# Gating the experts in transposed layout, with the gates of four chunks sent once through DRAM

## Chip, core and metric

The kernel runs on one core of one Trainium2 chip. The metric is the device time of one launch in microseconds (us). The engines are TensorE (PE: matmuls and transposes; PEld is its weight loads), VectorE (DVE), ScalarE (ACT), GpSimd (POOL) and SyncE (SP), which here only issues DMAs. DMAs are issued from SP's, ACT's and POOL's queues.

## The reference, cut to what matters

Attention over pooled keys, then two of eight low-rank experts per token. B=4, 12288 query tokens per batch, C=128, 768 pooled keys per batch, E=8 experts of rank 16.

```python
kv_pool = kv.reshape(B, H//4, 4, W//4, 4, C).mean(axis=(2, 4))
k = v = kv_pool.reshape(B, -1, C) @ w_sr
s = (q @ k.transpose(0, 2, 1)) / np.sqrt(C)
a = softmax(s);  x = (a @ v).reshape(-1, C)

logits = x @ w_gate                       # 8 experts, the best two kept
topk = np.argpartition(-logits, 2, axis=1)[:, :2]
w = softmax(logits of the two)
delta = sum over the two of  w * ((x @ A[e]) @ B[e])
return x + delta                          # (49152, 128) float32
```

## The kernel before, in words

The 49152 queries are cut into 96 chunks of 512 tokens (`T`), 24 chunks per batch, four chunks per group `g` of 2048 tokens (`GC`, `GT`). A chunk is four sub-tiles (`S`) of 128 tokens. The order of all instructions on each engine is the program's order (`keep`).

The main loop (L417) runs over slots `k` from 4 to 95. In slot `k`, PE computes the scores of chunk `k` in three parts (`scores`, L238: two matmuls of 512 columns each into one of two PSUM tiles `sg`), and ACT turns each part into `em` with one exp of 128x1024. The chunk before it is attended (`attend`, L248: 24 matmuls of 137 columns into `acc`, of which there is one buffer). The 137 columns are the 128 outputs, the 8 expert logits and the softmax sum. The chunk before that is normalised by DVE (`normalize`, L256: `rinv`, `xn`).

Then comes the expert part, or x stage, of a chunk. It needs `xn` and the gates of the chunk.

- Gates: for each group of chunks (`sizes`, L269: mostly four), DVE finds the sorted logits (`top`, L276), POOL makes `over`, ACT a tanh `th`, and POOL two more steps give `gw` (`route`, `gates`, L285 to L316). `gw` has tokens on partitions: 8 gates for each of the 16 sub-tiles.
- x stage: PE transposes `xn` of the chunk that enters, and in the same PSUM tile `hg` of the chunk that entered one slot before (`transposes`, L318: four and four matmuls of 128 columns); DVE copies both to `tts` (128x1024). `down` (L339) is four matmuls with the turned `x` as the weights and `a_bf` streaming, which puts tokens on partitions in `h_ps`. `gate` (L344, DVE) multiplies by `gw`, each gate broadcast over the 16 ranks of its expert. After the transpose of `hg` in the next slot, `up` (L353) is four matmuls into `d_ps`, one slot later again, and `finish` (L358, DVE) adds `xn` and issues the output DMA of 256 KB on SP.

The order of PE in a slot (L440 to L481) is: scores part 0, `transposes`, scores part 1, `up`, first quarter of `attend`, scores part 2, `down`, three quarters of `attend`. `tt_ps`, `h_ps`, `d_ps` and the tiles of the key preparation share two PSUM buffers (`mtile`).

Queries of groups 2 and up are cast to bf16 in DRAM by a DMA from POOL (`cast_q`, L77) and loaded transposed by a DMA transpose on SP (`load_qT`, L82). In such a group a sub-tile takes every sixteenth token, so that a partition's four output rows of a chunk lie side by side in DRAM. The keys and values of the next batch are loaded in slots 4 to 15 of a batch, 512 KB per slot (L430), summed by POOL in slots 10 to 20, and prepared in single steps (`rest`) in slots 14 to 23. A chunk enters the x stage as soon as its group's gates can be there (`enter`, L407 to L413); chunk 8 enters in slot 14. The last three chunks are finished in a tail written out by hand (L489 on).

Of the kernel before, what the change touches and what calls it, by code (L numbers as in the profile page):

```python
# [15 lines left out]
ALU = mybir.AluOpType  # L16
# [4 lines left out]
def kernel(  # L21
# [31 lines left out]
    qpool = ctx.enter_context(tc.tile_pool(name="qpool", bufs=4))  # L53
    ppool = ctx.enter_context(tc.tile_pool(name="ppool", bufs=7))
# [4 lines left out]
    opool = ctx.enter_context(tc.tile_pool(name="opool", bufs=6))  # L59
    qdram = ctx.enter_context(tc.tile_pool(name="qdram", bufs=1, space=bass.MemoryType.DRAM))  # L60
# [21 lines left out]
    def load_qT(g):  # L82
        t = qpool.tile([P, GT], BF16, tag="qT", name="qT")
        keep(nc.sync.dma_start(t.rearrange("c (j p) -> c j p", p=P),
                               q_bf[g].rearrange("(p j) c -> p (j c)", p=P), transpose=True))
        qT[g] = t
# [46 lines left out]
    keep(nc.sync.dma_start(b_f, moe_B.rearrange("e r c -> (e r) c")))  # L133
# [10 lines left out]
    nc.vector.tensor_copy(id_bf, id_f)  # L144
    wext = const.tile([P, VC], FP32)
# [89 lines left out]
    tts, xT, hgT, hp, hg, dp = {}, {}, {}, {}, {}, {}  # L235
    R = J // 2

    def scores(k, r):  # L238
# [7 lines left out]
        keep(nc.scalar.activation(em[k][:, 2 * r:2 * r + 2], ps, AF.Exp, bias=0.0, scale=scale))  # L246
# [22 lines left out]
    sizes = [1, 1, 2] + [GC] * (NCHUNK // GC - 5) + [2] * 4 + [1] * 8  # L269
# [13 lines left out]
    later = []  # L283
# [26 lines left out]
    def gates(k0, n, eng, arg, mask):  # L310
        th = rpool.tile([P, GC * S, 8], FP32, tag="th", name="th")[:, 0:n]
        keep(nc.scalar.activation(th, arg, AF.Tanh, bias=0.0, scale=0.5))  # L312
        w = gpool.tile([P, GC * S, 8], FP32, tag="gw", name="gw")
# [4 lines left out]
    def transposes(kx, kh):  # L318
# [14 lines left out]
        keep(nc.vector.tensor_copy(sb[:, lo:hi], ps[:, lo:hi]))  # L333
# [5 lines left out]
    def down(k):  # L339
        hp[k] = mtile([P, S, P], name="h_ps")  # L340
        for s in range(S):
            mm(hp[k][:, s], xT[k][:, s], a_bf, start=(s == 0), stop=(s == S - 1))

    def gate(k):  # L344
        k0, m = first[k], k - first[k]
        hg[k] = run.tile([P, S, P], BF16, tag="hg", name="hg")
        keep(nc.vector.tensor_tensor(  # L347
            hg[k].rearrange("p s (e r) -> p (s e) r", e=E),
            hp[k].rearrange("p s (e r) -> p (s e) r", e=E),
            gw[k0][:, m * S:(m + 1) * S].rearrange("p s e -> p (s e)")  # L350
            .unsqueeze(2).broadcast_to([P, S * E, RK]), op=ALU.mult))
# [5 lines left out]

    def finish(k):  # L358
        osb = opool.tile([P, S, C], FP32, tag="osb", name="osb")
        keep(nc.vector.tensor_tensor(osb, dp[k], xn[k][:, :, 0:C], op=ALU.add))  # L360
        keep(nc.sync.dma_start(
            out[k // GC * GT:(k // GC + 1) * GT].rearrange("(p j) c -> p j c", p=P)
            [:, k % GC * S:(k % GC + 1) * S], osb))
# [30 lines left out]
    keep(nc.vector.tensor_scalar(a_bf, a_f, 0.5, None, op0=ALU.mult))  # L394
# [12 lines left out]
    enter = {}  # L407
    e = 0
    for k in range(NCHUNK):
        done = normed[first[k] + size[k] - 1]  # L410
        two = size[k] < GC and k % 4 == 0 and len(enter.get(e, [])) < 2
        e = max(e if two else e + 1, done + 1)
        enter.setdefault(e, []).append(k)  # L413

    sums, rest = [], []
    kh, ku = [], []
    for k in range(LA, NCHUNK):  # L417
# [3 lines left out]
        if k % GC == 0:  # L421
            g = k // GC
            if 2 <= g + 1 < B * NG:
                load_qT(g + 1)
            if 4 <= g + 2 < B * NG and g + 2 not in q_bf:
                cast_q(g + 2)
        if b + 1 < B:
            if i == 4:
                sums, rest = prepare(b + 1, nc.gpsimd)
            if 4 <= i < 16:  # L430
                h, j = divmod(i - 4, 4)
                load_kv(b + 1, h, j, None)
# [12 lines left out]
        while later:  # L445
            later.pop(0)()
        for n in kn:
# [224 lines left out]
```

## Time and profile before

| what | value |
|---|---|
| time, median of 3 runs | 409.08 us (408.81 to 409.26) |
| the profiled execution, its own time | 409.56 us |
| its span on the core | 407.6 us |
| granted TensorE clock, mean | 0.991 |
| instructions | 11369 |
| DMA packets, bytes moved | 71319, 76.45 MB |
| share of SP's DMA queue / POOL's DMA queue in the time of 16 DMA engines | 53.8% / 16.7% |

The profiled execution took 2.0 us more than its span; that is start and end outside the core's first and last instruction. A timeline row gives the start in us from the span's start, the length, the engine, the line, the operation, output and input with their shapes, and the number of instructions merged into the row. PE's rows are pipelined: each ends later than the next one starts, so lengths on PE are read from start to start. The square bracket at the end of a row is the time for which the engine had been idle before it, and what ended that idle time.

### The profile page before, as it was taken

What the parts mean: (1) busy time and instruction counts of PE and PEld (TensorE: products, weight loads), DVE (VectorE), ACT (ScalarE), POOL (GpSimd) and SP (SyncE); (2) the same over time, 40 slices, a digit from 0 to 9 for tenths busy, and PEclk for the clock granted to TensorE, in tenths of its full rate; (3) what the DMA queues carried; (4) which work ended last, traced back from release to release, by engine and by line L of the source; (5) the groups of instructions that cost most, each with busy time, mean ns of one, the idle gap of its engine ahead of it and who ended that gap; (6) DMA issues with size and microseconds to landing.
All of it is one profiled execution on the core that took longest, in us unless ns stands there. A gap on an engine that the chain in (4) does not pass through costs nothing.

```text
span 407.6 us, 11369 instructions
## 1 busy us (share of the span) xinstructions
PE 379.6 (93%) x4514; PEld 306.9 (75%) x4589; DVE 324.5 (80%) x948; ACT 293.1 (72%) x346; POOL 170.7 (42%) x289
## 2 busy tenths in 40 slices
PE   3798899999999999999999999999999999898992
PEld 2556778788888788888888788878888878677781
DVE  2553678888888888989888888988988888887873
ACT  2389468767678777867778877876777877665772
POOL 0010128888512319879411319879311322123342
PEclk9999999999999999999999999999999999999996
DMA  8998568984855999994855979996756548252213
GB/s 297 366 265 245 137 156 214 285 210 124 182 130 105 307 172 336 295 219 138 168 130 117 363 103 344 287 225 145 156 131 149 138 130 156 79 138 97 79 53 132
DMA packets 71319, 76.45 MB, mean 188 GB/s; under 512 B 49921, under 2 KB 50433, under 8 KB 70785
## 3 DMA queue, kind: packets, MB, share of 16 engines
q1 hardware_dynamic: 70128, 63.98, 53.8%
q0 software_dynamic: 704, 11.54, 16.7%
q8 instruction: 36, 0.59, 0.6%
q10 hardware_dynamic: 432, 0.20, 0.2%
q14 instruction: 19, 0.15, 0.1%
HBM read 50.53 MB, written 36.70 MB: 214 GB/s over the span
## 4 chain that ended last, share of the span: by engine, by line
PE 82%; DVE 7%; ACT 3%; DMA 3%; issue 2%; SPq 1%; POOL 1%; ACTq 0%; DVEq 0%; POOLq 0%
PE acc L68 34%; PE sg L68 23%; PE tt_ps L68 10%; PE h_ps L68 6%; PE d_ps L68 5%; ACT em L246 2%; DVE rinv L258 1%; DVE xn L263 1%; DMA kvr<-in_kv_dram 1%; SPq L98 1%; DMA w_sr_sb<-in_w_sr_dram 1%; PE kpT_ps L68 1%; DVE tts L333 1%; PE v_ps L68 1%; DVE hg L347 1%
## 5 line engine op out<-in xcount | busy, mean ns | idle before, releaser
L246 ACT ACTIVATE em<-sg 128x1024 f16<-128x1024 f32 x288 | 279.1, 1023 | 92.1 <-PE sg L68 59.5
L68 PE MATMUL acc<-vx,em 128*128 128x137 f16 x2280 | 171.7, 224 | 1.7 <-DVE xn L263 1.6
L68 PE MATMUL sg<-qT,kfT 128*128 128x512 bf16 x501 | 154.7, 378 | 2.7 <-ACT em L246 2.2
L68 PEld LDWEIGHTS <-em 128*128 128x128 f16 x2304 | 149.6, 98 | 4.0 <-DVE xn L263 2.2
L68 PEld LDWEIGHTS <-tts 128*128 128x128 bf16 x740 | 56.4, 98 | 45.8 <-DVE tts L333 2.1
L293 POOL TENSOR_TENSOR over<-xn,srt 128x128 f32<-128x128 f32 (+2 forms) x62 | 21.4, 365 | 157.0 <-DVE srt L281 157.0
L347 DVE TENSOR_TENSOR hg<-h_ps,gw 128x512 bf16<-128x512 f32 x93 | 64.2, 691 | 13.2 <-POOL gw L315 7.6
L263 DVE TENSOR_TENSOR xn<-acc,rinv 128x544 f32<-128x544 f32 x95 | 68.8, 725 | 3.3
L333 DVE COPY tts<-tt_ps 128x1024 bf16<-128x1024 bf16 (+1 forms) x96 | 64.4, 671 | 3.6 <-PE tt_ps L68 3.6
L171 POOL TENSOR_TENSOR kvr<-kvr 128x512 f32<-128x512 f32 x54 | 66.7, 1271 | 0.0
L360 DVE TENSOR_TENSOR osb<-d_ps,xn 128x512 f32<-128x512 f32 x91 | 62.6, 691 | 0.5 <-PE d_ps L68 0.5
L68 PEld LDWEIGHTS <-kfT 128*128 128x128 bf16 x576 | 45.9, 97 | 6.0 <-issue 3.7
L68 PEld LDWEIGHTS <-xn 128*128 128x128 bf16 x384 | 29.4, 98 | 22.0 <-ACT xn L585 0.5
L258 DVE RECIPROCAL rinv<-acc 128x4 f32<-128x4 f32 x95 | 17.3, 182 | 32.5 <-PE acc L68 31.4
L68 PE MATMUL h_ps<-a_bf,tts 128*128 128x128 bf16 x372 | 36.0, 219 | 2.8 <-DVE tts L333 1.6
L68 PE MATMUL tt_ps<-id_bf,xn 128*128 128x128 bf16 x372 | 35.9, 219 | 1.5
L68 PE MATMUL d_ps<-b_bf,tts 128*128 128x128 bf16 x364 | 35.2, 219 | 2.3 <-DVE tts L333 1.3
L68 PE MATMUL tt_ps<-id_bf,hg 128*128 128x128 bf16 x368 | 35.6, 219 | 0.3 <-DVE hg L347 0.3
L281 DVE MAX8 srt<-xn 128x8 f32<-128x8 f32 x380 | 34.3, 153 | 0.2
L314 POOL TENSOR_TENSOR gw<-th,over 128x128 f32<-128x128 f32 (+2 forms) x31 | 12.0, 389 | 39.2 <-ACT th L312 39.1
L68 PEld LDWEIGHTS <-hg 128*128 128x128 bf16 x384 | 25.5, 98 | 2.5 <-issue 1.1
L169 POOL TENSOR_TENSOR kvr<-kvr 128x512 f32<-128x512 f32 (+1 forms) x18 | 18.1, 1006 | 0.9
(77 smaller groups left out, 174.8 us busy)
## 6 DMA issues: line engine op xcount, KB each, us to landing
out_dram<-osb SPq DMA_DIRECT2D x95, 256.0 KB, 3.3
kvr<-in_kv_dram SPq DMA_DIRECT2D x36, 512.0 KB, 6.3
qbf<-in_q_dram POOLq DMA_DIRECT2D x22, 512.0 KB, 6.1
kvr<-in_kv_dram SPq DMA_DIRECT2D x24, 256.0 KB, 5.4
qf<-in_q_dram SPq DMA_DIRECT2D x1, 1024.0 KB, 5.1
qf<-in_q_dram SPq DMA_DIRECT2D x4, 256.0 KB, 5.2
qT<-qbf SPq DMA_TRANSPOSE x22, 6.3
out_dram<-osb ACTq DMA_DIRECT2D x1, 128.0 KB, 3.1
```

The lines of the kernel that those rows point to most:

```text
L68: return keep(nc.tensor.matmul(*a, **k))
L169: keep(adder.tensor_tensor(u, u, v, op=ALU.add))
L171: keep(adder.tensor_tensor(u[:, lo:hi], u[:, lo:hi], v[:, lo:hi], op=ALU.add))
L246: keep(nc.scalar.activation(em[k][:, 2 * r:2 * r + 2], ps, AF.Exp, bias=0.0, scale=scale))
L258: keep(nc.vector.reciprocal(ri, acc[k][:, :, VC]))
L263: keep(nc.vector.tensor_tensor(x, acc[k][:, :, 0:VC], ri.unsqueeze(2).broadcast_to([P, S, VC]), op=ALU.mult))
L281: keep(nc.vector.max(srt[k0][:, m, s], xn[k][:, s, C:VC]))
L293: keep(eng.tensor_tensor(d, lg, so[:, :, i].unsqueeze(2).broadcast_to([P, n, 8]), op=ALU.subtract))
L314: keep(eng.tensor_tensor(w[:, 0:n], th, mask, op=ALU.mult))
L333: keep(nc.vector.tensor_copy(sb[:, lo:hi], ps[:, lo:hi]))
L347: keep(nc.vector.tensor_tensor(hg[k].rearrange("p s (e r) -> p (s e) r", e=E), hp[k].rearrange("p s (e r) -> p (s e) r", e=E), gw[k0][:, m ...
L360: keep(nc.vector.tensor_tensor(osb, dp[k], xn[k][:, :, 0:C], op=ALU.add))
```

## The change

For 18 groups of four chunks (chunks 8 to 79; `turned`) the x stage is made transposed:

- `down` becomes one matmul of 512 columns with `a_bf` as the weights, so that the 128 (rank, expert) pairs lie on partitions and tokens run along the row. `a_bf` and `b_f` are laid out rank first (`b_f` by eight DMAs of 16 rows on ACT's queue instead of one on SP's).
- `gate` multiplies `h_ps` by `gx`, the gates in the same layout, and writes `hgT`, which `up` takes as its weights in the next slot. The four transposes of `hg`, and its half of the copy to `tts`, are gone.
- `gx` is made once per group: POOL writes the gates as fp16 with expert before sub-tile (`gh`), PE transposes this one 128x128 tile (`turn_gates`, ahead of the last quarter of `attend`), DVE copies it to `gT`, a DMA on ACT's queue puts its 32 KB into DRAM in the next slot (`put_gates`), and in the slot after that a second DMA on ACT's queue loads it, spread over the 16 ranks, as 128 partitions x 2048 (`spread_gates`, 512 KB written). ACT waits for the first DMA before it issues the second.
- A chunk of these groups enters four slots after its group's last `normalize` (chunk 8 in slot 17). Slots 14 to 16 have no x stage. In slots 82 to 95, 20 chunks enter where 17 did before; two chunks enter in slots 82, 84, 86, 87, 88 and 91, and the second one's copy to `tts` is made by ACT. The other 24 chunks keep the old form, with the gate broadcast along the rank-first layout.
- `load_qT` takes 16 rows of 128 tokens in place of 128 rows of 16. The exp of chunks 8 and up therefore reads its PSUM tile in another order (`ps.rearrange`), with a step of 64 elements (256 B) between neighbours, and writes `em` without gaps, so that a partition still has four adjacent output rows.
- Keys and values are loaded in pieces of 256 KB, two per slot at first and then one per slot, from slot 4 on through the whole kernel; `cast_q` and `load_qT` run one group further ahead. The pools of `qT` and `em` shrink from 4 to 3 and from 7 to 6 buffers.

```diff
-        t.rearrange("c (j p) -> c j p", p=P),
-               q_bf[g].rearrange("(p j) c -> p (j c)", p=P), transpose=True))
+        t.rearrange("c (j r) -> c j r", r=16),
+               q_bf[g].rearrange("(r j) c -> r (j c)", r=16), transpose=True))
...
-    keep(nc.sync.dma_start(b_f, moe_B.rearrange("e r c -> (e r) c")))
+    for e in range(E):
+        keep(nc.scalar.dma_start(b_f[e::E], moe_B[e]))
...
-        keep(nc.scalar.activation(em[k][:, 2 * r:2 * r + 2], ps, AF.Exp, bias=0.0, scale=scale))
+        o = em[k][:, 2 * r:2 * r + 2]
+        if k // GC > 1:
+            ps = ps.rearrange("p i (j s r) -> p i s r j", s=S, r=16)
+            o = o.rearrange("p i (s r j) -> p i s r j", s=S, r=16)
+        keep(nc.scalar.activation(o, ps, AF.Exp, bias=0.0, scale=scale))
...
-    sizes = [1, 1, 2] + [GC] * (NCHUNK // GC - 5) + [2] * 4 + [1] * 8
+    sizes = [1, 1, 2, 2, 2] + [GC] * (NCHUNK // GC - 6) + [2] * 4 + [1] * 8
...
+        if k0 in turned:
+            keep(eng.tensor_tensor(th, th, mask, op=ALU.mult))
+            gh[k0] = gpool.tile([P, P], FP16, tag="gh", name="gh")
+            keep(eng.tensor_tensor(gh[k0].rearrange("p (e s) -> p s e", e=E), th, mask, op=ALU.add))
+            turns.append(k0)
+            return
...
+    def turn_gates(k0):
+        ps = mtile([P, P], FP16, name="gT_ps")
+        mm(ps, gh[k0], id_h, is_transpose=True, start=True, stop=True)
+        sb = gtpool.tile([P, P], FP16, tag="gT", name="gT")
+        keep(nc.vector.tensor_copy(sb, ps))
+        return sb
+
+    def put_gates(k0, sb):
+        gt[k0] = gdram.tile([P, P], FP16, tag="gt", name="gt")
+        keep(nc.scalar.dma_start(gt[k0], sb))
+
+    def spread_gates(k0):
+        gx[k0] = gxpool.tile([P, GT], FP16, tag="gx", name="gx")
+        keep(nc.scalar.dma_start(gx[k0], gt[k0].rearrange("(e s) t -> e (s t)", e=E)
+                                 .unsqueeze(0).broadcast_to([RK, E, GT])))
...
     def down(k):
         hp[k] = mtile([P, S, P], name="h_ps")
+        if k in turned:
+            mm(hp[k], a_bf, xT[k], start=True, stop=True)
+            return
...
     def gate(k):
+        if k in turned:
+            hgT[k] = run.tile([P, S, P], BF16, tag="hgT", name="hgT")
+            keep(nc.vector.tensor_tensor(
+                hgT[k], hp[k], gx[k0][:, m * T:(m + 1) * T].rearrange("p (s t) -> p s t", s=S),
+                op=ALU.mult))
+            return
...
+    TURN = 4
+    ready = {k: normed[first[k] + size[k] - 1] + (TURN if k in turned else 1) for k in range(NCHUNK)}
+    enter, t, left = {}, LA, list(range(NCHUNK - 3))
+    while left:
+        can = [k for k in left if ready[k] <= t]
+        many = t >= NCHUNK - 14 and t < NCHUNK - 2 and t % 5 and len(can) > 1
+        enter[t] = can[:2] if many else can[:1]
...
+        while nload < min(24 * (B - 1), k + 8, 2 * (k - LA) + 2):
+            bn, n = divmod(nload, 24)
+            load_kv(bn + 1, n // 8, n % 8 // 2, n % 2)
+            nload += 1
+        if k % GC == 1 and g + 2 < B * NG:
+            load_qT(g + 2)
...
         scores(k, 0)
         while later:
             later.pop(0)()
+        for k0, (since, sb) in list(turning.items()):
+            if k == since + 1:
+                put_gates(k0, sb)
+            else:
+                spread_gates(k0)
+                turning.pop(k0)
...
         for a_ in ka[-1:]:
             for s in range(1 if len(ka) == 1 else 0, S):
+                if s == S - 1:
+                    for x_, h_ in pairs[1:]:
+                        transposes(x_, h_, nc.scalar)
+                        kd = [x_] if x_ is not None else []
+                    for k0 in turns:
+                        turning[k0] = k, turn_gates(k0)
+                    turns.clear()
                 attend(a_, s)
-        ku = kh
-        kh = kx
+        ku = kh + [x_ for x_ in kx[:1] + kdone if x_ in turned]
+        kh = [x_ for x_ in kx[:1] + kdone if x_ not in turned]
+        kdone = kd
```

## The prediction

> **What bounds the kernel now.** I read the page's busy shares first, then a table of busy time by stage, the timeline of one slot in the steady part, and the DMA issues with their time to landing.
>
> ```profile
> PE 379.6 (93%) x4514; PEld 306.9 (75%) x4589; DVE 324.5 (80%) x948; ACT 293.1 (72%) x346; POOL 170.7 (42%) x289
> 100.00:120.00 20.00, 19.79 (x245) 16.31 (x248) 17.76 (x52) 15.13 (x18) 7.20 (x12) 1.00 0.79 170
> 360.00:380.00 20.00, 17.99 (x224) 14.42 (x226) 16.31 (x48) 13.55 (x17) 5.81 (x22) 1.00 0.27 86
> ```
>
> The stage rows give busy us of PE, PEld, DVE, ACT and POOL. From 60 to 340 us PE is busy for 19.79 of every 20 us at clock 1.00: it sets the pace. In the tail it is 18 of 20.
>
> ```profile
> 158.79 0.59 PE L68 MATMUL sg<-qT,kfT 128*128 128x512 bf16 x2
> 159.20 0.72 DVE L263 TENSOR_TENSOR xn<-acc,rinv 128x544 f32<-128x544 f32 x1
> 159.22 0.39 PE L68 MATMUL tt_ps<-id_bf,xn 128*128 128x128 bf16 x4
> 159.44 0.39 PE L68 MATMUL tt_ps<-id_bf,hg 128*128 128x128 bf16 x4
> 159.48 2.87 ACT L246 ACTIVATE em<-sg 128x1024 f16<-128x1024 f32 x3 [0.81 <-PE sg L68]
> 159.66 0.59 PE L68 MATMUL sg<-qT,kfT 128*128 128x512 bf16 x2
> 159.86 0.69 DVE L333 COPY tts<-tt_ps 128x1024 bf16<-128x1024 bf16 x1
> 160.09 0.39 PE L68 MATMUL d_ps<-b_bf,tts 128*128 128x128 bf16 x4
> 160.32 0.54 PE L68 MATMUL acc<-vx,em 128*128 128x137 f16 x6
> 160.52 0.69 DVE L360 TENSOR_TENSOR osb<-d_ps,xn 128x512 f32<-128x512 f32 x1
> 160.69 0.59 PE L68 MATMUL sg<-qT,kfT 128*128 128x512 bf16 x2
> 161.12 0.39 PE L68 MATMUL h_ps<-a_bf,tts 128*128 128x128 bf16 x4
> 161.35 1.28 PE L68 MATMUL acc<-vx,em 128*128 128x137 f16 x18
> 161.55 0.69 DVE L347 TENSOR_TENSOR hg<-h_ps,gw 128x512 bf16<-128x512 f32 x1
> 162.47 0.38 PE L68 MATMUL sg<-qT,kfT 128*128 128x512 bf16 x1
> ```
>
> One slot is 162.47 - 158.79 = 3.68 us, with no bracket on a PE row. Start to start: scores pair 0.43, transposes of `xn` 0.22 and of `hg` 0.22, `up` 0.23, quarter of attend 0.37, `down` 0.23, the rest of attend 1.12. ACT needs 2.87 and idles 0.81. DVE needs 0.18 + 0.72 + 0.69 + 0.69 + 0.36 (four maxima) + 0.69 = 3.33.
>
> ```profile
> out_dram<-osb SPq DMA_DIRECT2D x95, 256.0 KB, 3.3
> kvr<-in_kv_dram SPq DMA_DIRECT2D x36, 512.0 KB, 6.3
> qbf<-in_q_dram POOLq DMA_DIRECT2D x22, 512.0 KB, 6.1
> ```
>
> The last number is the median us from issue to landing; the new gate transfers are priced from these rows.
>
> **Part by part.** *Removed on PE.* The `hg` transposes (0.22), and one 512-column matmul (half of a scores pair, 0.215) for four of 128 (0.23): 0.235 per chunk, 72 chunks, -16.9 us. *Added:* one gate transpose per group, a quarter of 0.22: 18 x 0.055 = +1.0. If nothing else changed, a slot would be 3.45.
>
> *A new limit, scores part 2 against the exp.* Part 2 reuses the PSUM tile that the exp of part 0 reads. Today part 2 starts 160.69 - 158.79 = 1.90 after part 0; the exp starts 0.69 after it and takes 1.023 (its group's mean), so it ends at 1.71, hidden. The `hg` transposes lay in that stretch: without them PE is there at 1.68. Where PE already waits for this exp, early in the run (PE at 32.05, exp at 32.68, PE again at 33.76 after "0.24 <-ACT em"), the distance is 1.71. Bounds of the stall 0.03 (that row) and 0.09 (1.71 plus 0.06 of signal, less 1.68). I take 0.05, nearer the row that shows a stall: 72 x 0.05 = +3.6.
>
> *The strided exp.* It now steps 256 B in PSUM. No long strided PSUM read is in the trace. Nearest rows: the contiguous exp, 1.023, and PE's transposes of `xn`, which read every second bf16 from SBUF, 219 ns against 219 for the dense `hg`: no penalty. Upper bound, from the dense exp: its price again, 2.05. I take 1.023; the stride costs 0 then, and the other end is a rival.
>
> The Trainium skill speaks against this ("SBUF — State Buffer", the note on SBUF cachelines within "Door 1: The DMA port swizzle"): PSUM has lines of 8 bytes, and a non-contiguous pattern in it significantly slows matmuls. By that rule, if it held for ACT's reads as well, the sum would end well above the time before; the page states no number for ACT, and no row here shows one.
>
> *Gates on POOL and PE.* `gw` in the timeline is ready 3.05 us into its slot (slot from 151.43; tanh 153.04, then two POOL steps of 0.46, end 154.48). `gh` takes the same two steps, the second writing fp16 with gaps. PE wants it before the last quarter, at 3.50 - 0.37 = 3.13. What waits behind it on PE is that quarter, the next scores, and with them ACT. Bounds 0 (the 3.05 holds) and 0.35 (the second step at 0.74, the row of POOL's 128x256 add): I take 0.1, near the first row. 18 x 0.1 = +1.8.
>
> *DVE.* `tts` falls from 0.69 to 0.41 (the 128x512 form, at 39.68 us), `gT` adds at most 0.28 (the 128x256 `kfT` copy) per four slots: 3.12 of 3.50 us, hidden. `xn` ends 159.92 - 158.79 = 1.13 into the slot, attend's first quarter now comes at 0.43 + 0.22 + 0.43 + 0.23 = 1.31: 0.12 is left after 0.06 of signal, so anything that delays `rinv` by more costs PE directly.
>
> *ACT.* Three exps at 2.87, two DMA issues per four slots (0.36 to 0.45 in ACT's rows), one tanh of 0.3: 12.6 of 14.0 us per group, hidden.
>
> *The two DMAs.* The put is issued after the exp of part 0, 0.69 + 0.96 = 1.65 into its slot, the spread in the same place a slot later: ACT waits only if the put takes over 3.5 us. Behind it stand exps 1 and 2, then PE's scores; ACT's idle time covers 0.5 us of it. Bounds for landing are output rows of 256 KB: least 2.0, longest 8.8, median 3.1. I take under 3.5, cost 0. The spread must be in when DVE gates chunk one, 2.6 into the next slot; DVE has 0.4 of room and `acc` 0.1. So from 1.65 to 3.5 + 3.1: about 5.0 us. If it is later, `gate` holds DVE's queue: `rinv` and `xn` behind it, then attend, PE. Landing is bounded by quiet 256 KB outputs (2.3 between 370 and 405 us, so about 3.1 for twice the bytes) and by the 512 KB `kvr` row, 6.3, which includes waiting in SP's queue. The nearest row is `qbf`, alone on its queue: 6.1, of which it keeps 16 engines busy for 0.167 x 407.6 / 22 = 3.1 us; 512 KB cost 0.54 x 407.6 x 0.52 / 64 = 1.8 at SP's rate. 6.1 - 3.1 + 1.8 = 4.8: just in time, with a spread (4.7 to 9.5 for `qbf`). I take 0.15 late on average, 18 x 0.15 = +2.7; ends 0 and 1.3 x 18 = 23.4. The extra 10 MB raise the DMA share from 71% by about 54% x 10 / 64 = 8 points, less than the 1.00 to 1.11 at which `kvr` loads ran from 140 to 180 us without loss on PE.
>
> In the Trainium skill ("DMA: Bandwidth & Descriptors", "Anatomy of one DMA — SWDGE (gpsimd) path") a DMA issued by GpSimd costs about 2.0 us plus its bytes at 436 GB/s. Carried over to ACT's queue that is an estimated 3.2 us for the spread, and the sum would be 2.7 us lower; but by it a 512 KB `kvr` load would be 3.2 as well, and the row says 6.3.
>
> *Queues and buffers.* SP gets 36 more issues at 0.55 us, one per slot, beside transposes of 2.3 to 7.0: per group 3.9 + 4 x 0.55 + 4 x 0.34 = 7.5 of 14 us. `qT` is asked for seven slots ahead, over 20 us against 9.5 at worst; six `osb` cover late outputs; POOL's casts move one group earlier, not more of them. Without that cover a late `qT` would stop PE. ACT's eight `b_f` issues (8 x 0.43 = 3.4 us) push the table load from 1.66 to about 5, done at 6.6; its first copy is at 8.56. Pools of 3 and 6: the buffer taken was last read at least one slot before. Cost 0, with a microsecond either way.
>
> *Moved work.* Slots 14 to 16 lose an x stage: PE 3.68 - 0.90 = 2.78, so ACT's 2.87 sets them, 0.1 lost each. Three x stages go to the tail, where a slot with two keeps DVE at 3.33 + 0.69 + 0.69 = 4.7 against PE's 3.68 + 0.9 = 4.6: three more such slots at 0.1 to 0.3. Together +1.0; ends -1 and +4.
>
> Sum: -16.9 + 1.0 + 3.6 + 1.8 + 2.7 + 1.0 = -6.8. The profiled execution took 409.56 (span 407.6 and 1.96 around it): 402.8. It stands 0.5 above the median of the runs, 409.08, so on that scale **402.3 us**.
>
> **Rivals.** *All of it arrives:* slots at 3.45, the gates always in time: 409.08 - 16.9 + 1.0 = 393.2, with the moved work 394. For it: PE's unbroken rows. Against: 1.68 lies below 1.71, and the gates end 0.1 before PE wants them.
>
> *The spread lands late (slower):* at `gate` of each group's first chunk DVE waits, and PE after it, one for one beyond 5.0 us. At 6.3, the `kvr` median, 402.3 - 2.7 + 23.4 = 423. It decides at (6.8 + 2.7) / 18 = 0.53 late, a landing of 5.5. For it: both rows of that size stand above 6, and in the spread's slot a cast is issued too. Against: a queue of its own, 256 KB pieces in place of 512.
>
> *The strided read costs:* in 88 chunks each 0.1 us more per exp delays scores part 2 by as much: 88 x 0.1 = 8.8, which ends the gain (402.3 becomes 411). Doubled, three exps of 1.96 bind at 5.9 per slot: 402 + 88 x (5.9 - 3.5) = 613. For it: no such row. Against: the read of every second bf16 at no cost.
>
> **Chances.** The forecast (396 to 408) 0.58; all of it 0.14; a spread about 5.5 us that evens out 0.05; later than that 0.17; a costly stride 0.06. Under 0.2% can't be told from no change here. Faster 0.72, same 0.05, slower 0.23. The range, 393.5 to 414, takes in the whole saving and a spread landing at 5.8 us; beyond both ends lie about 0.2.
>
> **What would show it.** Steady slots of 3.48 to 3.54 with "<-ACT em" on scores part 2; exp means at 1.02; no bracket "<-POOL gh" above 0.35 on the gate transpose; `gx` landing below 5.0, and no wait for `gx` on DVE. I am wrong if the exp's mean is above 1.1, if DVE waits for `gx` by over half a us per group, or if ACT waits for the put.

## The result: 453.2 us against 409.05, slower by 9 per cent

The changed kernel took 453.24 us (median of 4 runs, 444.29 to 459.21), the kernel before 409.05 us on the same chip; the ratio is 1.092, 95% interval 1.082 to 1.103. The forecast was 402.3 us with a range of 393.5 to 414. The profiled execution took 457.19 us with a span of 455.4. The changed kernel's runs differ by 3 per cent, and disturbed ones are left out of the ratios, which can therefore lie below the quotient of the medians.

The page's busy shares and its slices of the changed kernel:

```profile
PE 389.6 (86%) x4037; PEld 294.4 (65%) x4103; DVE 306.4 (67%) x959; ACT 299.6 (66%) x356; POOL 172.0 (38%) x295
...
PE   3598899957986987999986986979997999999992
...
PEclk9689999997998998999998998889999999999996
```

PE has gaps all along its row, and the clock digit falls at several of them. The chain of work that ended last names what ended the gaps; its first line here is of the kernel before, the other two of the changed one:

```profile
PE 82%; DVE 7%; ACT 3%; DMA 3%; issue 2%; SPq 1%; POOL 1%; ACTq 0%; DVEq 0%; POOLq 0%
...
PE 54%; DMA 27%; DVE 10%; ACT 4%; issue 2%; POOL 1%; SPq 0%; DVEq 0%; ACTq 0%; POOLq 0%
PE acc L71 23%; DMA gx<-gt 16%; PE sg L71 15%; DMA gt<-gT 6%; PE h_ps L71 4%; PE tt_ps L71 4%; DMA kvr<-in_kv_dram 3%; PE d_ps L71 3%; DVE xn L273 3%; ACT em L256 3%; PE kpT_ps L71 2%; DVE osb L412 2%; DVE hgT L387 1%; DMA w_sr_sb<-in_w_sr_dram 1%; DVE rinv L268 1%
```

Both gate transfers stand in it: 16% for the spread (`gx<-gt`), 6% for the put (`gt<-gT`). The wait table gives the engines that stood, with us in total, times, and the longest:

```profile
DVE hgT L387 <- DMA gx<-gt: 35.7, 12, 8.7
...
PEld L71 <- DVE hgT L387: 24.2, 8, 6.6
...
ACT em L256 <- DMA gt<-gT: 12.5, 4, 3.6
```

And the page's DMA issues, the last number being the median us from issue to landing:

```profile
gx<-gt ACTq DMA_DIRECT2D x18, 512.0 KB, 5.7
...
gt<-gT ACTq DMA_DIRECT2D x18, 32.0 KB, 3.7
```

The spreads landed after 4.5 to 11.9 us, the puts after 1.4 to 7.5.

One undisturbed slot of the changed kernel's timeline runs from 151.52 to 155.05:

```profile
151.52 0.59 PE L71 MATMUL sg<-qT,kfT 128*128 128x512 bf16 x2
...
153.28 0.59 PE L71 MATMUL sg<-qT,kfT 128*128 128x512 bf16 x2
...
155.05 0.38 PE L71 MATMUL sg<-qT,kfT 128*128 128x512 bf16 x1
```

It takes 3.53 us (3.68 before). The next group's turn looks different, in the same view:

```profile
161.57 0.58 POOL L82 DMA_DIRECT2D qbf<-in_q_dram  x1
...
161.97 0.10 PEld L71 LDWEIGHTS <-gh 128*128 128x128 f16 x1 [0.26 <-POOL gh L327]
...
163.19 0.33 ACTq L344 DMA_DIRECT2D gt<-gT  x1
...
170.54 6.41 SPq L87 DMA_TRANSPOSE qT<-qbf  x1
170.68 0.53 ACTq L348 DMA_DIRECT2D gx<-gt  x1
171.25 1.94 ACT L256 ACTIVATE em<-sg 128x1024 f16<-128x1024 f32 x2 [3.59 <-DMA gt<-gT]
172.33 1.01 PE L71 MATMUL sg<-qT,kfT 128*128 128x512 bf16 x2 [2.69 <-ACT em L256]
...
178.96 0.69 DVE L387 TENSOR_TENSOR hgT<-h_ps,gx 128x512 bf16<-128x512 f32 x1 [2.90 <-DMA gx<-gt]
```

Read it as a chain. POOL has made the gates and issues the next cast at once (161.57). The put follows at 163.19, and the trace's packets show that its first one started only at 167.66, when half of the cast's 16 (163.54 to 169.31) were over. It landed after 7.5 us, so ACT, in whose queue the spread waits for the put, issued the spread late (170.68) and stood 3.59 us with two exps behind it, which PE then missed for 2.69. The late spread now left beside the transpose of `qT` (170.54), landed at 178.9, and DVE waited another 2.90 us for it.

In six of the 18 groups the cast leaves 1.6 to 1.8 us before the put, as here; five of these puts took 6.6 to 7.5 us, the sixth, late in the run (370.99), 4.7. In the others, where key sums stand on POOL between the gates and the cast or the put comes later, the put took 1.4 to 4.2. Of VectorE's 35.7 us, 19.0 fall in those five groups and 8.7 in the first group. Another 6 fall in two groups whose put landed in 1.5 us, but where the cast left 0.3 and 1.0 us before the spread (issued at 291.51 and 310.53): there the spread itself, beside the cast, took 8.6 and 7.8 us.

The clock pays as well. Three stretches of the changed kernel, the undisturbed slot, the stall, and a part of the stall; the columns are the length, busy us of PE, PEld, DVE, ACT and POOL, the granted clock, the DMA share and GB/s:

```profile
151.52:155.05 3.53, 3.53 (x42) 2.65 (x40) 2.90 (x9) 2.85 (x4) 0.00 (x0) 1.00 0.89 239
170.50:180.00 9.50, 6.37 (x50) 4.15 (x50) 2.52 (x10) 7.11 (x8) 2.44 (x6) 0.82 0.88 233
...
172.00:175.00 3.00, 2.67 (x14) 1.56 (x14) 0.42 (x1) 2.56 (x4) 0.00 (x0) 0.50 1.08 281
```

Over the 9.5 us of the stall the clock is 0.82 in the mean where it was 1.00, and right after the pause it is 0.50: the pair of scores matmuls takes 1.01 us there instead of 0.59.

The start of `rinv` per chunk is the ledger. Its first column is the kernel before (us), the others are the differences of other kernels to it, each read from one profiled execution; the columns after the first difference belong to the experiments (runs 1, 3, 6, 8 and 18).

| chunk | before | changed | one load of `b_f` | no transport | no casts | more time | run 18 |
|---|---|---|---|---|---|---|---|
| 0 | 32.2 | +6.2 | -0.5 | +4.7 | +5.0 | +5.0 | -0.3 |
| 12 | 75.3 | +6.3 | -0.2 | +4.8 | +5.0 | +5.1 | -0.1 |
| 16 | 90.8 | +13.5 | +7.4 | +3.8 | +7.4 | +3.9 | -1.3 |
| 24 | 122.2 | +21.0 | +14.2 | +2.4 | +5.9 | +3.8 | -2.7 |
| 48 | 213.2 | +32.3 | +30.8 | -0.1 | +3.2 | +2.4 | -5.1 |
| 64 | 272.9 | +46.1 | +42.5 | -1.5 | +1.7 | +2.5 | -6.6 |
| 84 | 350.1 | +46.8 | +46.2 | -4.2 | -1.0 | +1.6 | -8.0 |
| 95 | 394.6 | +47.6 | +47.0 | -3.5 | -0.2 | +5.2 | -5.5 |

The loss has two parts: 6.2 us before the first chunk, and some 42 us in steps at the heads of groups, between chunks 12 and 72. After chunk 72 it does not grow.

For the first part, the timeline of the start:

```profile
1.67 6.15 ACTq L137 DMA_DIRECT2D b_f<-in_moe_B_dram  x8
6.22 3.91 SPq L101 DMA_DIRECT2D kvr<-in_kv_dram  x6
```

And what SP's queue waited for:

```profile
SPq L101 <- DMA w_sr_sb<-in_w_sr_dram: 5.1, 1, 5.1
```

The first load of keys is issued at 6.22 us (before: 1.19) because it waits for `w_sr`, which it does not read. In the built program the DMAs of SP and ACT count on eight completion counters, dealt in turn; with seven more loads the turn is back at `w_sr`'s counter when it comes to SP's first `kvr`, which then waits until that counter is free. Before, the first five `kvr` loads had no wait.

### The profile page after: what moved, and what is told of

Its sections match the earlier page's. It is cut to its first block, busy times and chain, and to the rows that moved or that the text cites. A ratio compares the mean times of both kernels' runs of the same rounds, so it can differ in the third digit from the quotient of the medians.

```text
span 455.4 us, 10622 instructions
## 1 busy us (share of the span) xinstructions
PE 389.6 (86%) x4037; PEld 294.4 (65%) x4103; DVE 306.4 (67%) x959; ACT 299.6 (66%) x356; POOL 172.0 (38%) x295
## 4 chain that ended last, share of the span: by engine, by line
PE 54%; DMA 27%; DVE 10%; ACT 4%; issue 2%; POOL 1%; SPq 0%; DVEq 0%; ACTq 0%; POOLq 0%
PE acc L71 23%; DMA gx<-gt 16%; PE sg L71 15%; DMA gt<-gT 6%; PE h_ps L71 4%; PE tt_ps L71 4%; DMA kvr<-in_kv_dram 3%; PE d_ps L71 3%; DVE xn L273 3%; ACT em L256 3%; PE kpT_ps L71 2%; DVE osb L412 2%; DVE hgT L387 1%; DMA w_sr_sb<-in_w_sr_dram 1%; DVE rinv L268 1%
## 5 line engine op out<-in xcount | busy, mean ns | idle before, releaser
L256 ACT ACTIVATE em<-sg 128x1024 f16<-128x1024 f32 x288 | 280.5, 1025 | 130.9 <-PE sg L71 76.8
L71 PE MATMUL acc<-vx,em 128*128 128x137 f16 x2280 | 180.5, 228 | 4.8 <-DVE xn L273 4.8
L71 PEld LDWEIGHTS <-em 128*128 128x128 f16 x2304 | 157.0, 100 | 21.2 <-DVE xn L273 7.7
L387 DVE TENSOR_TENSOR hgT<-h_ps,gx 128x512 bf16<-128x512 f32 x72 | 49.8, 691 | 45.6 <-DMA gx<-gt 35.7
L369 DVE COPY tts<-tt_ps 128x512 bf16<-128x512 bf16 (+1 forms) x88 | 41.0, 466 | 13.4 <-PE tt_ps L71 13.3
L71 PEld LDWEIGHTS <-hgT 128*128 128x128 bf16 x288 | 21.9, 99 | 40.6 <-DVE hgT L387 24.2
L71 PE MATMUL d_ps<-b_bf,hgT 128*128 128x128 bf16 x288 | 28.6, 223 | 21.1 <-DVE hgT L387 20.5
L71 PE MATMUL h_ps<-tts,a_bf 128*128 128x512 bf16 x72 | 28.2, 392 | 1.6 <-issue 0.2
L71 PEld LDWEIGHTS <-tts 128*128 128x128 bf16 x164 | 12.1, 98 | 11.1 <-issue 1.9
L325 POOL TENSOR_TENSOR th<-th,over 128x128 f32<-128x128 f32 x18 | 8.2, 456 | 20.9 <-ACT th L323 19.3
L71 PE MATMUL kpT_ps<-id_f,kvr 128*128 128x128 f32 x66 | 12.9, 334 | 3.4 <-DVE kvr L181 3.4
```

What stands on the lines that cost most here:

```text
L71: return keep(nc.tensor.matmul(*a, **k))
L256: keep(nc.scalar.activation(o, ps, AF.Exp, bias=0.0, scale=scale))
L325: keep(eng.tensor_tensor(th, th, mask, op=ALU.mult))
L387: keep(nc.vector.tensor_tensor(hgT[k], hp[k], gx[k0][:, m * T:(m + 1) * T].rearrange("p (s t) -> p s t", s=S), op=ALU.mult))
```

## The experiments

All are the changed kernel with the edits shown; each ratio refers to runs of the kernel before on the same chip.

| run | median us | ratio to before, 95% |
|---|---|---|
| 1 one load of `b_f` | 450.5 | 1.087 to 1.095 |
| 2 old layout of `qT` | 467.5 | 1.118 to 1.126 |
| 3 no transport of the gates | 406.4 | 0.992 to 0.995 |
| 4 TURN 5 | 441.2 | 1.074 to 1.086 |
| 5 casts in 4 KB packets | 444.4 | 1.078 to 1.089 |
| 6 no casts | 409.6 | 0.999 to 1.005 |
| 7 plain loads for transposes | 436.2 | 1.055 to 1.061 |
| 8 more time on both legs | 418.6 | 1.015 to 1.025 |
| 9 casts behind the spread | 427.0 | 1.038 to 1.048 |
| 10 the same, one load of `b_f` | 422.6 | 1.030 to 1.035 |
| 11 the same, TURN 5 | 426.4 | 1.037 to 1.046 |
| 12 casts after routing, one load | 427.9 | 1.035 to 1.044 |
| 13 the same, first group by the old path | 432.2 | 1.021 to 1.027 |
| 14 run 8, one load of `b_f` | 414.5 | 1.006 to 1.014 |
| 15 the same, transpose a slot later | 410.7 | 1.002 to 1.006 |
| 16 the same, casts in 4 KB packets | 407.0 | 0.992 to 0.997 |
| 17 spread on SP, TURN 5, one load | 405.4 | 0.987 to 0.990 |
| 18 the same, casts in 4 KB packets | 404.0 | 0.987 to 0.991 |

**Run 1: the start alone.**

```diff
-    for e in range(E):
-        keep(nc.scalar.dma_start(b_f[e::E], moe_B[e]))
+    keep(nc.sync.dma_start(b_f, moe_B.rearrange("e r c -> r e c")))
```

> Only change against the changed kernel: b_f is loaded by one DMA on SyncE's queue again (rows in the new order) instead of eight on ScalarE's. Theory A (the eight small loads hold the first kv loads of SyncE back, whose first one issues at 6.22 us where it was 1.19): that issue returns to 1 to 2 us, the first rinv from 38.5 us to 32 to 33, and the time falls by about 6 us, to 438 to 453, with the waits for the gates unchanged at some 36 us on VectorE and 12 on ScalarE. Rival (the late start is of the moved a_f, the fp16 identity or the clock): the first rinv stays at 38 to 39 and the time at 444 to 459.

The mechanism held: the first `kvr` left at 1.20 us, the first `rinv` came at 31.8. The time did not follow: the interval of the ratio, 1.087 to 1.095, lies inside that of the changed kernel. The ledger has the 6.7 us gained at chunk 0 and only 0.6 of it at the end, because the waits for `gx` grew from 35.7 to 42.5 us. A gain ahead of stalls that hang on how transfers fall together need not survive them.

**Run 2: the transpose's packets.** One DMA transpose moves 16 packets of 32 KB in the changed kernel, 2048 of 256 B before.

```diff
-        keep(nc.sync.dma_start(t.rearrange("c (j r) -> c j r", r=16),
-                               q_bf[g].rearrange("(r j) c -> r (j c)", r=16), transpose=True))
+        keep(nc.sync.dma_start(t.rearrange("c (j p) -> c j p", p=P),
+                               q_bf[g].rearrange("(p j) c -> p (j c)", p=P), transpose=True))
```

> Only the layout of qT is put back: the DMA transpose reads 2048 pieces of 256 B as in the kernel before instead of 16 pieces of 32 KB, exp and the stores go back with it, the gates still travel through DRAM. Theory B (the long packets of the transposes hold the gates' DMAs back): the spreads land within 5 us of their issue in nearly all groups (median 5.7, longest 11.9 now), VectorE's wait for gx falls from 35.7 us to under 12, and the time to 415 to 432. Rival C (the casts' 32 KB packets, which stay, hold them): the puts stay late in 6 or 7 groups, ScalarE's wait for gt stays near 12 and the time falls by less than 12 us, to 435 to 450. Rival D (the number of DMAs or their completion counters, not the packets): nothing changes, 444 to 459.

None of the three theories had it slower: 467.5 us. One spread, issued 0.03 us after a transpose and with a cast beside it, took 39.0 us to land. With gates and casts beside it, the layout of before is the worse one; the transpose's long packets are not what the gates lose by.

**Run 3: no transport.**

```diff
     def put_gates(k0, sb):
+        return
...
     def spread_gates(k0):
+        gx[k0] = g_any
```

> The gates are still made, turned and copied to SBUF, but not sent: put and spread are left out, and every gate step multiplies by one constant tile, so that the gated sums are of wrong gates. If the transport of the gates is the whole of the stalls at the heads of the groups (some 49 us by the starts of rinv), the profiled time falls from 457 to 402 to 412, where the late start of 6.2 us is still in it. If the stalls come of something else (the gates' turn on TensorE, the x stage nine slots on, kv loads in halves), more than 425 us are left.

406.4, and the chain that ended last has 3% of DMA, as in the kernel before: the stalls at the heads of groups are the transport's, all of them. The late start of 4.7 us is still in it, and from chunk 0 to 95 this kernel gains 8.2 us on the one before.

**Run 4: one more slot for the spread.**

```diff
-    TURN = 4
+    TURN = 5
```

> TURN is 5 instead of 4: the gated chunks enter one slot (some 3.5 us) later, nothing else moves. Theory (the spread simply has too short a time; its landing does not depend on the slot): VectorE's wait for gx falls from 35.7 us to 8 to 12 (only the four groups that waited over 3.5 us keep the rest), ScalarE's wait of 12.5 us for the put's landing stays, and the time falls by 24 to 32 us, to 415 to 433. Rival (what the spread waits for moves with the work): the wait stays over 20 us and the time above 438.

VectorE's wait for `gx` fell to 5.0 us, as expected, but the time was 441.2, above the range: DMA `gt<-gT` stands with 13% in the chain of this run, and ten puts of 18 took over 5 us. The more slack is given to the second leg, the more the first shows, and it holds ACT.

**Run 5: short cast packets.**

```diff
-        keep(nc.gpsimd.dma_start(t, q[g // NG, (g % NG) * GT:(g % NG + 1) * GT]))
+        src = q[g // NG, (g % NG) * GT:(g % NG + 1) * GT]
+        keep(nc.gpsimd.dma_start(t.rearrange("(a b j) c -> b a (j c)", a=2, j=16),
+                                 src.rearrange("(a b j) c -> b a (j c)", a=2, j=16)))
```

> Only the casts of q to bf16 are cut into short packets: 256 pieces of 4 KB (as written) instead of 16 of 32 KB; same bytes, same time of issue. Theory F (the put of the turned gates waits behind one cast packet of 3 us and one transpose packet of 2.6 us on its DMA engine, because GpSimd issues a cast right after it has made the gates): the longest put falls from 7.5 us to under 5, ScalarE's wait for gt from 12.5 us to under 5, and the time by 10 to 25 us, to 425 to 440. Rival G (short packets hold the engines no less, as the 256 B packets of the old transpose did): the puts stay late and the time is 444 or more.

444.4, and its interval overlaps that of the changed kernel, so a gain is not shown. ScalarE still waited 10.7 us for `gt`; the longest put was 7.1. So it is not a single long packet in front. With 4 KB packets the put of one group (issued at 155.49) still began at 159.19, while the cast's packets ran from 156.26 to 161.97.

**Run 6: no casts.**

```diff
         if k % GC == 0 and 4 <= g + 3 < B * NG:
-            cast_q(g + 3)
+            q_bf[g + 3] = q_bf[2 + (g + 3) % 2]
```

> The casts of groups 4 to 23 are left out; their transposes read the two cast groups 2 and 3 in turn, so that the scores are of wrong queries. Theory F (the casts are what makes the put late): the puts land within 4.5 us, ScalarE's wait for gt is under 4 us, VectorE's wait for gx under 20, and the time is 415 to 432. Rival (the transposes, the kv loads and the stores on SyncE's queue are enough for it): the waits stay at over 35 us together and the time above 437.

409.6, below the theory's range. VectorE's wait for `gx` was 7.1 us, 4.3 of it at the first group. The DMA issues of this run:

```profile
gx<-gt ACTq DMA_DIRECT2D x18, 512.0 KB, 5.2
...
gt<-gT ACTq DMA_DIRECT2D x18, 32.0 KB, 2.6
```

With transport but without casts the loss is gone, as it is with casts but without transport: the two together make it. After the first group every put landed within 4.1 us. This run also takes the casts' bytes off the DMA engines; runs 9 to 13, which keep the casts and move them, tell the one from the other in part.

**Run 7: plain loads in place of the transposes.**

```diff
-        keep(nc.sync.dma_start(t.rearrange("c (j r) -> c j r", r=16),
-                               q_bf[g].rearrange("(r j) c -> r (j c)", r=16), transpose=True))
+        keep(nc.sync.dma_start(t, q_bf[g].rearrange("(p j) c -> p (j c)", p=P)))
```

> The DMA transposes are replaced by plain loads of the same 512 KB in rows of 4 KB at the same places, so that the scores are of wrong queries; casts, kv loads and gates' transport stay. Theory H (what makes the spread late is that a transpose is issued beside it): the spreads land in at most 6.5 us, VectorE's wait for gx falls from 35.7 us to under 15, and the time to 418 to 436; the put, which waits for the cast, stays late. Rival (a plain load of the same bytes is as much in the way): the wait stays over 25 us and the time above 440.

Between the theory and its rival: 436.2 lies at the end of the theory's range, but the wait for `gx` stayed at 28.9 us and spreads still took up to 8.5. The transposes seem to have a part in it, not the main one.

**Run 8: more time on both legs.**

```diff
-    gxpool = ctx.enter_context(tc.tile_pool(name="gxpool", bufs=2))
+    gxpool = ctx.enter_context(tc.tile_pool(name="gxpool", bufs=3))
...
-    TURN = 4
-    ready = {k: normed[first[k] + size[k] - 1] + (TURN if k in turned else 1) for k in range(NCHUNK)}
+    TURN = 6
+    ready = {k: normed[first[k] + size[k] - 1] + ((TURN if k < 72 else 5) if k in turned else 1) for k in range(NCHUNK)}
...
-            else:
+            elif k == since + 3:
                 spread_gates(k0)
```

> More time for the gates on both legs: the gated chunks enter two slots later (TURN 6 up to chunk 71, 5 for the last turned group), the spread is issued one slot later, so that ScalarE finds the put landed, and gx has three buffers. If the cost is only that two transfers of up to 7.5 and 12 us have 3.6 and 5 us of room, both waits go to nearly 0, and the time falls to 406 to 413, with the late start of 5 to 6 us still in it. If the transport also costs through what it takes from the other transfers (kv loads, stores, qT late), some 10 us or more remain: 417 to 435.

418.6, at the low end of the second case. VectorE waited 5.6 us for `gx`, and ScalarE's wait for `gt` is no longer in its table, though the spreads landed later than in the changed kernel (5.4 to 10.8 us, thirteen of them over 8). The ledger has what is left: 5.0 us at the start, and 3.6 between chunks 84 and 95, probably where the chunks that entered late are caught up with (2.5 with TURN 5 in run 18, 0.8 with TURN 4 in the changed kernel).

**Runs 9, 10 and 11: the cast held until the spread is in.**

```diff
-        if k % GC == 0 and 4 <= g + 3 < B * NG:
+        if k % GC == 0 and 4 <= g + 3 < min(7, B * NG):
             cast_q(g + 3)
+        if k % GC == 1 and 7 <= g + 3 < B * NG:
+            keep(nc.gpsimd.tensor_copy(late, gx[max(gx)][:, 0:1]))
+            cast_q(g + 3)
```

> The casts stay whole, but each is issued about five slots-quarters later: GpSimd first copies one column of the gx that is landing, so that the cast starts when the spread is in and not beside the next put. Theory F (a cast that is issued just after the gates are made holds the DMA engines for 3 to 4 us in front of the put, and so makes the spread late too, into the transpose): the puts land within 5 us, ScalarE's wait for gt is under 4 us (12.5 now), VectorE's wait for gx under 12 (35.7), and the time is 408 to 418, close to the 409.6 without casts. Rival (the cast then runs into the transpose of qT or the kv loads, which are late instead): TensorE waits for qT or the next put is late as before, 425 or more.

> The casts behind the spread, and b_f in one DMA on SyncE's queue. Theory: with the waits gone the 6 us that the start gains (first rinv 32 us instead of 38) are no longer taken back at the heads of the groups as they were with the single load alone: 402 to 411, so not slower than the kernel before. Rival (the waits take back what is gained elsewhere): within 2 us of the run without the single load.

> As the last one, with TURN 5: one more slot for the spread. If what is left of VectorE's wait for gx is some 5 to 12 us, it goes: 400 to 408. If nothing is left of it, no change beyond 2 us; if TURN 5 costs something itself (buffers held longer, the end of the program), slower.

Run 9: 427.0, 26 us below the changed kernel by the medians and 20 by the ratios, but not the 408 to 418 expected. Puts fell to at most 5.3 us and VectorE's wait for `gx` to 15.4. Run 10 was 4.5 us faster and still slow, and its profiled execution keeps only 0.8 of the 5.8 us by which its start is earlier than run 9's; its waits say why:

```profile
POOL late L478 <- DMA gx<-gt: 121.1, 17, 12.7
...
DVE hgT L386 <- DMA gx<-gt: 19.0, 9, 7.1
...
ACT th L322 <- POOL over L308: 17.7, 7, 5.4
```

My edit made POOL stand 121 us before `gx`; the key sums and the routing behind it came late, and ACT, in its own order, waited 17.7 us for the routing's `over`. Run 11 with TURN 5 was slower still, though VectorE's wait was 4.3.

**Runs 12 and 13: the cast after the routing, without a wait.**

```diff
         for n in kn:
             after_norm(n)
+        if k % GC == 1 and 7 <= g + 3 < B * NG:
+            cast_q(g + 3)
...
-    sizes = [1, 1, 2, 2, 2] + [GC] * (NCHUNK // GC - 6) + [2] * 4 + [1] * 8
+    sizes = [1, 1, 2, 2, 2, 2, 2] + [GC] * (NCHUNK // GC - 7) + [2] * 4 + [1] * 8
```

As in run 9, the casts of groups 7 and up no longer stand at slots 0 mod 4. `sizes` is run 13's alone.

> As the run with the casts behind the spread and one load of b_f, but GpSimd does not wait for gx: the cast is simply issued after the four routing operations of the slot, some 3.5 us before the next put. Theory (the 13 us that were left there were mostly my own wait: GpSimd stood 121 us before gx, so that routing came late, ScalarE waited 17.7 us for over and the put came late): ScalarE's wait for over falls under 5 us, VectorE's wait for gx under 15, and the time to 404 to 415. Rival (a cast anywhere near the put is in its way): the put stays over 4.5 us in most groups and the time above 418.

> As the one before, and the first group of four (chunks 8 to 11) is routed in two pairs by the old path, so that the first spread comes 15 us later, when the kv loads of the start (two per slot) are through. Theory (the first spread, which waited 4 to 8 us in every run with transport, is late because of these loads): the wait at the first turned group falls under 1.5 us and the time is 3 to 6 us below the run before. Rival (the first turned group is late wherever it is): no change beyond 1.5 us.

Run 12: ScalarE's wait for `over` fell to 3.4 us as the theory had it, but VectorE's for `gx` was 22.1 and the time 427.9, the rival's, though only seven of the 18 puts took over 4.5 us. A cast 3.6 to 4.2 us ahead of the put can still be in its way: such puts took 3.4 to 6.9 us. Run 13: the first turned group, now chunks 12 to 15, still waited 6.3 us, so the loads of the start are not needed for its lateness. But here a cast left 3.6 us before its put and a transpose 0.3 us before its spread. Why the first group is late without casts too (over 7 us for its spread in run 6) stays open.

**Runs 14 to 16: slack, mended start, transposes out of the way.** Run 14 is run 8 with run 1's edit; run 15 issues the transpose in slots 2 mod 4; run 16 adds run 5's packets.

```diff
-        if k % GC == 1 and g + 2 < B * NG:
+        if k % GC == 2 and g + 2 < B * NG:
             load_qT(g + 2)
```

> The version with more time for both legs (TURN 6, spread one slot later, three gx buffers), with b_f in one DMA on SyncE's queue; the casts stay where they were. Theory: where nothing waits for the gates, what the start gains stays gained, unlike in the run with the single load alone: first rinv 5 us earlier, and the time 4 to 7 us under the 418.6 of the version without it, 409 to 415. Rival (the waits take it back): within 2 us of 418.6.

> As the one before, with the transpose of qT issued one slot later (chunks 2 mod 4), after the spread and not beside it. Theory (spread and transpose issued together cost the spread 3 to 4 us: they land after 8 to 11 us where the spread alone takes 4.5): the spreads land in under 7 us, what was left of VectorE's wait for gx (5.6 us) goes, 405 to 411. Rival (transpose and put then collide): ScalarE waits for gt again, no gain.

> As the last version (TURN 6, late spread, one load of b_f, transpose one slot later; 410.7), with the casts in 4 KB packets. If short cast packets let the gates pass sooner, as the 10 us of the run with short packets alone suggest, VectorE's wait for gx (7.9 us) goes and the time is 406 to 409.5. If only lateness counts and the slack already hides it, 409.5 to 412.

Run 14: 4.1 us under run 8, as its theory had it. That the start's gain stays is not as clear as that: VectorE's wait for `gx` rose from 5.6 to 9.1 us, and the two profiled executions end 1.1 us apart, where their starts differ by 5.2. Run 15 gained 3.8 more by the medians, 2.3 by the ratios, but not by the theory's way: spreads still landed after 4.4 to 11.8 us, VectorE's wait was 7.9. Run 16 gained 3.7 again, and with it the kernel is half a per cent below the one before; the wait for `gx` was 2.6.

**Runs 17 and 18: the spread on SP's queue.**

```diff
-            if k == since + 1:
-                put_gates(k0, sb)
-            else:
-                spread_gates(k0)
-                turning.pop(k0)
+            put_gates(k0, sb)
+            spread_gates(k0)
+            turning.pop(k0)
...
-        keep(nc.scalar.dma_start(gx[k0], gt[k0]...
+        keep(nc.sync.dma_start(gx[k0], gt[k0]...
...
-    TURN = 4
+    TURN = 5
```

> TURN 5 and one load of b_f; the spread is issued on SyncE's queue right behind the put's issue, so that it starts when the put lands and not at a slot's start, and ScalarE never waits for it; stores and kv loads stand behind it instead. Theory (the gates need about 10 to 14 us from the put's issue and have 12 before they are wanted; the rest was waiting for slots and ScalarE standing): ScalarE's wait for gt is 0, VectorE's for gx under 15, and the time is 403 to 412. Rival (stores, kv loads and transposes behind the blocked queue are late): waits for osb buffers or kvr, 415 or more.

> The last version (spread on SyncE's queue, TURN 5, one load of b_f; 405.4) with the casts in 4 KB packets as well. If the waits that it has left (VectorE 3.9 us for gx) and the spread of its times (403.8 to 411.5) are of the casts' long packets, 402.5 to 405 and a narrower spread; if not, 404 to 407.

Run 17: 405.4. Its timeline on SP at one group, and two rows of its wait table, SP's own and VectorE's:

```profile
141.27 3.81 SPq L412 DMA_DIRECT2D out_dram<-osb  x1
145.13 0.59 SPq L101 DMA_DIRECT2D kvr<-in_kv_dram  x1
145.81 0.56 SPq L347 DMA_DIRECT2D gx<-gt  x1
...
SPq L347 <- DMA gt<-gT: 31.0, 9, 7.6
...
DVE hgT L386 <- DMA gx<-gt: 3.9, 2, 2.7
```

The put was issued at 139.62 and landed 6.1 us later, at 145.70; the spread left then, not at a slot's start, and though it took 7.1 us itself, VectorE waited 1.1. In 15 of the 18 groups the spread left within 0.15 us of the put's landing. SP's queue stood 31.0 us for it in the whole run without harm: VectorE's wait for `gx` is 3.9 us, ScalarE's for `gt` is not in the table, and VectorE waits 2.1 us for `kvr` (2.5 in run 1). Run 18 took 404.02 us (403.64 to 406.65), ratio 0.989, 0.987 to 0.991; the two intervals overlap, so the short packets of run 18 are not shown to matter for the time here, though VectorE's wait for `gx` is 0.3 us in its profile. Its puts still took up to 7.3 us: a cast delays them with either length of packet. The page of run 18:

```profile
PE 372.5 (93%) x4036; PEld 283.6 (71%) x4103; DVE 307.0 (76%) x958; ACT 299.0 (74%) x357; POOL 173.8 (43%) x295
...
PE   3798899999999999999999999999999999998992
...
PE 72%; DVE 10%; ACT 6%; issue 3%; POOL 3%; DMA 3%; SPq 1%; POOLq 0%; ACTq 0%; DVEq 0%
```

The gaps are gone and DMA has 3% of the chain, where it had 27%. So the version that beats both kernels, the one before by 1.1 per cent, is the changed kernel with one load of `b_f`, the spread on SP and one more slot.

## Why the prediction was wrong

- *Slot, new limit, strided exp: right.* A slot of 3.48 to 3.54 was forecast, 3.53 measured; part 2 of the scores starts 153.28 - 151.52 = 1.76 after part 0, 0.05 after that exp's end (152.21 + 1.02), so the wait for the exp costs 3.53 - 3.45 = 0.08, inside 0.03 to 0.09. The exp's mean is 1025 ns (1023 before), by the rows below: the stride costs nothing. The rule of the Trainium skill weighed against it ("SBUF — State Buffer", "Door 1: The DMA port swizzle") speaks of matmuls, and ACT's reads here do not follow it.

```profile
L246 ACT ACTIVATE em<-sg 128x1024 f16<-128x1024 f32 x288 | 279.1, 1023 | 92.1 <-PE sg L68 59.5
...
L256 ACT ACTIVATE em<-sg 128x1024 f16<-128x1024 f32 x288 | 280.5, 1025 | 130.9 <-PE sg L71 76.8
```

- *Gates on POOL and PE: mechanism right, size low.* The second POOL step takes 0.75 us, the upper row, and a slot with a turn 3.84, 0.31 more than the others; 0.26 of it is the wait for `gh` in the bracket at 161.97. The two terms were 1.0 + 1.8 = 2.8 us; by this slot they are 18 x 0.31 = 5.6.
- *The sum without the transport: right within the error.* -6.8 less the 2.7 for the spread is -9.5; run 3 gains 8.2 from the first chunk to the last.
- *The two DMAs: wrong, and nearly the whole miss.* The put was taken to land "under 3.5, cost 0"; its median was 3.7 and its longest 7.5. The spread was taken to be late by 0.15 us on average, +2.7 us in all, ends 0 and 23.4 us; with the put it cost 453.2 - 406.4 = 47 us by the medians, (1.092 - 0.993) x 409 = 40 by the ratios. Both signs of being wrong came: DVE waited 35.7 / 18 = 2.0 us per group, and ACT waited 12.5 us for the put. The step that failed is where each transfer was priced by medians of rows of transfers by themselves, on "a queue of its own". Even the row that was to bound the put said more: its median of 3.1 takes in the quiet tail, and from 60 to 340 us 42 of the 74 output stores took over 3.5. (The 4.7 to 9.5 given for `qbf` takes in the transposes that read it; the casts alone took 5.4 to 8.9. And the put and the spread left 0.77 us into their slots, 163.19 - 162.42 and 152.29 - 151.52, not 1.65, which gave the spread more time than the sum had.) The text placed a cast in the spread's slot; but the timeline of before has one right behind the gates:

```profile
139.30 0.46 POOL L315 TENSOR_TENSOR gw<-gw,over 128x128 f32<-128x128 f32 x1
139.70 0.58 POOL L79 DMA_DIRECT2D qbf<-in_q_dram  x1
```

  Wherever no key sums stand between, POOL issues the cast as it finishes the gates, and so beside the put. And it summed a lateness per group on DVE alone, where a late put first holds ACT, then moves the spread beside the transpose, then holds DVE, and costs clock on top.
- *The rival that lands late* had the right place and sign (423, against 453 measured, with a chance of 0.17), and its point of decision, a landing of 5.5 us, was close to the median of 5.7. It left out the put and what the two do to each other.
- *ACT's eight `b_f` issues: wrong.* They were costed at 0 because the first copy at 8.56 us would hide them on ACT. The cost, 6.2 us, came on SP, through the counters that both queues share.
- *qT's new layout at 0:* not shown wrong; putting the old one back made it worse (run 2).

## What to carry to other kernels

A transfer between two engines' work is priced by what else is issued in the same few microseconds on every queue, not by its own queue: list, slot by slot, which DMAs the other queues start there, and look at the longest landing of such rows and not the median. An instruction that waits for a DMA must not stand in the queue of an engine that has other work to do; move it to a queue that can stand still, and it starts when its input lands instead of at a slot's start. A saving in the steady part is worth measuring with the suspected stall cut out first (run 3): it tells at once whether the idea or its delivery is at fault.

## What the runs showed of the hardware

- While a cast from POOL's queue ran, packets of the other queues hardly started. In run 18 the records of one cast (a record is what the profile lists as one packet), 128 of 4 KB, run from 139.56 to 142.25; the put, issued at 138.31, started its first packet at 142.00, and SP's queue, on which four stores and loads had been issued from 138.52 on, started none of its 2 KB packets from 139 to 142 and 173 in the microsecond after. In the changed kernel the same is seen with records of 32 KB: from 164.0 to 167.0, with the cast of 163.54 running, SP's queue started 16 of its 2 KB packets, against 203 from 161.0 to 162.5.
- The Trainium skill has a rule for it ("DMA: Bandwidth & Descriptors", "Queues, rings and completion order"): a DMA engine takes turns between its queues, but finishes a whole packet of up to 64 descriptors from one before it turns to the next. The eight 4 KB records that a cast has per engine in run 5 would be one such packet, which agrees with the median of the puts there: 4.9 us, no earlier than the 3.7 with records of 32 KB. A cast cut into several DMAs, which would tell, was not run.
- A put of 32 KB keeps the 16 DMA engines busy for 0.15 us (128 packets of 0.019 us, changed kernel) and lands in 1.45 us where nothing is beside it; beside a cast it took up to 9.6 (run 15).
- With 256 B packets, a DMA transpose with a cast and a spread beside it can stall all three: run 2's 39 us, in which the DMA engines read as busy while little moved (DMA share 1.37 at 38 GB/s from 110 to 120 us). It is one case, and its cause stays open.
